# First pair of batches: copies of M1 on VectorE, two thirds of the early sums over w_in on GpSimd

## The chip, the cores and the metric

The kernel runs on one core of a Trainium2 chip. The core has a matrix engine (TensorE), three engines for elementwise work (VectorE, ScalarE, GpSimd) and a queue engine (SyncE); each works through its own list of instructions in order and waits on semaphores for the others. The metric is the device time of one execution in microseconds (us); smaller is better. The time shown is the median of repeated runs; the profile is of one further execution.

## The reference

The kernel computes an attention with a sigmoid in place of a softmax, and then a feed-forward block with SiLU:

```python
scores = q @ k.T / sqrt(64) - log(448)          # batch 8, heads 12, seq 448, head_dim 64
attn   = sigmoid(scores) @ v
x      = attn, heads side by side               # 3584 tokens x 768
h      = x @ w_in                               # w_in  768 x 2048
out    = (h * sigmoid(h)) @ w_out               # w_out 2048 x 768
```

Inputs and output are float32. The kernel works in float16 with float32 accumulation.

## The kernel before, in words

The order of the instructions is written out by hand; no scheduler moves them. What the program emits first on an engine runs first on that engine.

**Attention.** Batches are taken in pairs. A group `g` is a set of four heads of one batch (24 groups, three per batch). For each group `scores(g, ch)` (L210) computes one of seven chunks of scores in a double bank of PSUM (`psc`, two of them), and ScalarE turns it into `attnT` with a sigmoid. `values(g)` (L232) multiplies the seven chunks with v into two single banks (`pav`, from a pool of four), and VectorE moves them out as `xT`, scaled. k and q have to be transposed first: for groups 0 to 5 on TensorE, with copies by VectorE (`kT`, `qT`), later by DMA from copies `kr`, `qr`.

**Feed-forward.** For a pair of batches `h = x @ w_in` is a 2x2 block product by a seven-product scheme (Strassen's, Winograd's form): products M1 to M7 of sums of blocks of x (`tx`, by VectorE in `x_sums`, L336) and sums of blocks of w_in. The latter are four blocks, SI1, SI2, SI4 and SI3 (the last written over a block of w_in itself), each made in four quarters of its columns by `w_in_sums` (L318). `out` is made the same way, with sums over w_out (`w_sum`, L521), two of them by GpSimd behind a one-element copy (`gate`) that holds them until the last `tx` is there.

**The first pair.** The change lies here. The first 24 chunks of scores run with the work that the table `behind` places behind them. From chunk 24 on, `burst(n)` (L772) does two chunks of scores and, when a group is complete, its values; behind each burst `fill` takes a counted number of steps from `first_fill` (L603). Those steps are the part of the feed-forward that needs only the first batch: two plain columns (`h_unit`), then for columns 2 to 7 the products M1 and M2, then two plain columns again. M1 and M2 of one column share a bank: `early_m1` (L383) computes M1 and a copy of it is kept in `m1s` (L392), `early_m2` (L395) adds M2 on top, so M2 cannot start before the copy is done. Then ScalarE makes `sig` and VectorE writes `gTr` (`to_sig`, L278), which frees the bank. Between the bursts `next(in_sums)` emits one of the sums over w_in at a time, as `sums_behind` (L792) counts them: quarters 1, 2 and 3, twelve sums; quarter 0, whose columns are still needed, follows in `sets`, far later. After the last burst `last_part_of` (L803) begins the values of group 5 in new banks, and `first_pair` (L484) does the rest of the products.

**Loads.** All loads of q, k, v and weights go through GpSimd's queue (`load`, L112), in the order of the program: a load that has to wait for its buffer, or for one of eight transfers in flight, holds what stands behind it, loads and arithmetic alike. Buffers for groups are three deep, so k and q of group 8 take those of group 5. `after_transpose` (L679) and `after_values` (L691) say behind which step a load is emitted.

Of the kernel before, what the change touches and what calls it, by code (L numbers as in the profile page):

```python
# [13 lines left out]
AF = mybir.ActivationFunctionType  # L14
# [4 lines left out]
def kernel(  # L19
# [9 lines left out]
    nc = tc.nc  # L29
# [13 lines left out]
    NQB = NQ * B  # L43
# [41 lines left out]
    def one_bank(name):  # L85
        if "any" in banks:
            ring.append(ring.pop(0))
            return banks["any"].tile([P, 512], F32, tag=f"any{ring[-1]}", name=name)
        taken.append(name)
        return banks["single"].tile([P, 512], F32, tag="single", name=name)  # L90
# [12 lines left out]
    def new_flat(name, g):  # L103
        flat[name, g] = p3.tile([P, 2, NCH, D], F16, tag=f"{name}f", name=f"{name}f")

    def rows_in(name, g):
        b, iq = divmod(g, NQ)
        return source[name][b, 4 * iq : 4 * iq + 4].rearrange(
            "(i h) (p c) d -> (h p) i (c d)", h=2, c=NCH
        )  # L110

    def load(names, g, c0=0, c1=NCH):  # L112
        for name in names:
            if (name, g) not in flat:
                new_flat(name, g)
            nc.gpsimd.dma_start(  # L116
                flat[name, g][:, :, c0:c1].rearrange("p i c d -> p i (c d)"),
                rows_in(name, g)[:, :, c0 * D : c1 * D],
            )
# [144 lines left out]
    def first_col(m):  # L264
        return P if m % 2 == 0 else 0
# [12 lines left out]
    def to_sig(ph, to):  # L278
        if "sig" not in rooms:
            rooms["sig"] = [  # L280
                cpool.tile([P, 2, S], F16, tag=f"S{i}", name="sig") for i in range(1, 5)
            ]
            rooms["sig"] = [t[:, j] for j in range(2) for t in rooms["sig"]]
        tsig = rooms["sig"].pop(0)
        rooms["sig"].append(tsig)
        nc.scalar.activation(tsig, ph, AF.Sigmoid, bias=0.0, scale=ISX)
        nc.vector.scalar_tensor_tensor(  # L287
            out=to, in0=ph, scalar=ISX, in1=tsig, op0=ALU.mult, op1=ALU.mult
        )

    def h_unit(b, fc):
# [20 lines left out]
    wi = [  # L312
        [w_in_sb[:, c * NQ : (c + 1) * NQ, r * NH : (r + 1) * NH] for c in range(2)]
        for r in range(2)
    ]
    si = {3: wi[1][0]}

    def w_in_sums():  # L318
        for i in (1, 2, 4):
            si[i] = cpool.tile([P, NQ, NH], F16, tag=f"SI{i}", name=f"SI{i}")  # L320
        quarter = NH // 4
        add, sub = nc.vector.tensor_add, nc.vector.tensor_sub
        for at in (1, 2, 3, 0):
            cols = slice(at * quarter, (at + 1) * quarter)
            for op, o, x, y in (
                (add, si[1], wi[1][0], wi[1][1]),
                (sub, si[2], si[1], wi[0][0]),
                (sub, si[4], wi[0][1], si[2]),
                (sub, si[3], wi[0][0], wi[1][0]),
            ):  # L330
                op(o[:, :, cols], x[:, :, cols], y[:, :, cols])  # L331
                yield
# [19 lines left out]
    def products(m):  # L352

        x0 = xT[2 * m]
        col = first_col(m)
        bank, got = {}, {}

        def scratch():
            return p12.tile([P, S], F32, tag="attnT", name="part")

        def silu(i, r, c, h):
            nc.scalar.activation(  # L362
                gTr[:, r * NG + i, col + c * S : col + (c + 1) * S], h, AF.Silu, bias=0.0, scale=ISX
            )

        def steps(i, to, w, x, start=True):
            for n in range(NQ):
                nc.tensor.matmul(  # L368
                    to,
                    w[:, n, i * P : (i + 1) * P],  # L370
                    x[:, n],
                    start=(start and n == 0),
                    skip_group_check=not start,
                    stop=(n == NQ - 1),
                )
                if n < NQ - 1:
                    yield

        def product(*what, **how):
            for _ in steps(*what, **how):  # L380
                pass

        def early_m1(i):  # L383
            bank[i, "a"] = one_bank("pa")[:, :S]
            yield from steps(i, bank[i, "a"], wi[0][0], x0[:, :NQ])
            if "m1" not in rooms:
                rooms["m1"] = [
                    cpool.tile([P, NQ, 512], F32, tag=f"T{t}", name="m1s") for t in (2, 4)
                ]
                rooms["m1"] = [t[:, n, :S] for t in rooms["m1"] for n in range(NQ)]  # L390
            got[i, 1] = rooms["m1"].pop(0)
            nc.scalar.activation(got[i, 1], bank[i, "a"], AF.Copy)  # L392
            yield

        def early_m2(i):  # L395
            yield from steps(i, bank[i, "a"], wi[0][1], x0[:, NQ:], start=False)
            to_sig(bank[i, "a"], gTr[:, i, col : col + S])
            yield

        def plus(o, po, x):  # L400
            nc.vector.tensor_add(o, po, x)  # L401

        def m1(i):
            bank[i, "a"] = one_bank("pa")[:, :S]
            product(i, bank[i, "a"], wi[0][0], x0[:, :NQ])
            got[i, 1] = scratch()
            nc.scalar.activation(got[i, 1], bank[i, "a"], AF.Copy)  # L407

        def m2(i):
            product(i, bank[i, "a"], wi[0][1], x0[:, NQ:], start=False)  # L410

        def silu11(i):
            silu(i, 0, 0, bank[i, "a"])

        def m6(i):
            b = one_bank("pb")[:, :S]
            product(i, b, si[2], tx[m, 2])
            got[i, "u2"] = scratch()
            plus(got[i, "u2"], b, got.pop((i, 1)))

        def m5(i):
            bank[i, "d"] = one_bank("pd")[:, :S]
            product(i, bank[i, "d"], si[1], tx[m, 1])

        def m7(i):
            bank[i, "c"] = one_bank("pc")[:, :S]
            product(i, bank[i, "c"], si[3], tx[m, 3])
            got[i, "u3"], got[i, 22] = scratch(), scratch()
            plus(got[i, "u3"], bank[i, "c"], got[i, "u2"])

        def h22(i):
            plus(got[i, 22], bank[i, "d"], got.pop((i, "u3")))

        def m4(i):
            product(i, bank[i, "c"], wi[1][1], tx[m, 4], start=False)
            plus(bank[i, "c"], bank[i, "c"], got[i, "u2"])
            silu(i, 1, 0, bank[i, "c"])

        def m3(i):
            product(i, bank[i, "d"], si[4], xT[2 * m + 1][:, NQ:], start=False)  # L440
            plus(bank[i, "d"], bank[i, "d"], got[i, "u2"])
            silu(i, 0, 1, bank[i, "d"])

        def silu22(i):
            silu(i, 1, 1, got.pop((i, 22)))

        return SimpleNamespace(**locals())
# [231 lines left out]
    def after_transpose(g):  # L679
        if g == 0:  # L680
            load("kq", 3)
        elif g == 1:
            load("kq", 4)
            load_w_in(0)
            load_w_in(1)
        elif g == 2:
            load("kq", 5)
        elif g == 5:
            load("kq", 8)

    def after_values(g):  # L691
        if g == 0:
            load("v", 3)
            load_w_in(2)
            load_w_in(3)
        elif g == 1:
            load("v", 4)
            load_w_out(0, 0)
            load_w_out(0, 1)
        elif g == 2:  # L700
            load("v", 5)
            load_w_out(1, 0)
            load_w_out(1, 1)
            load("kq", 6)
            load("kq", 7)
        elif g + 3 < NQB:
            load("v", g + 3)
        if g % (2 * NQ) == 2 * NQ - 2:
            x_sums(g // (2 * NQ), 0, NQ - 1)
# [18 lines left out]
    def transposes(g, name):  # L728
        pe_transpose(g, ((name, 0, 4), (name, 4, NCH)))
        if name == "q":  # L730
            after_transpose(g)
# [53 lines left out]
    def fill(stream, n):  # L785
        for _ in range(n):
            next(stream, None)
# [1 line left out]
    first = products(0)  # L789
    stream = first_fill(first)  # L790
    behind_burst = {24: 6, 26: 4, 28: 4, 30: 4, 32: 7, 34: 7, 36: 4, 38: 7, 40: 3}
    sums_behind = {32: 2, 34: 2, 36: 3, 38: 3, 40: 2}  # L792
    fill(stream, 6)
    for n in range(NT_B + 3, 2 * NT_B, 2):
        burst(n)
        if n in (26, 30):
            transposes(5, "k" if n == 26 else "q")
        for _ in range(sums_behind.get(n, 0)):
            next(in_sums)
        fill(stream, behind_burst[n])  # L800
    assert next(stream, 0) == 0

    def last_part_of(g, m, then):  # L803
# [95 lines left out]
```

## Time and profile before

| | us |
|---|---|
| median of 3 runs | 385.35 (384.96 to 385.90) |
| profiled execution | 387.63 |
| its span, first to last instruction | 385.80 |
| TensorE busy | 365.8 (95%) |
| VectorE busy | 262.2 (68%) |
| ScalarE busy | 258.4 (67%) |
| GpSimd busy | 90.5 (23%) |

In the profile PE is TensorE, PEld its loading of weights, DVE VectorE, ACT ScalarE, POOL GpSimd and SP SyncE. A line such as `PE pa L368 <- ACT m1s L392: 3.4, 2, 1.9` says that TensorE, at line 368, waited for ScalarE's writing of m1s at line 392: 3.4 us in all, two times, the longest 1.9. Rows of a timeline give start, duration, engine, line, operation and its output and input. Where several instructions follow each other on one engine, the next often starts before the last has fully ended, so 0.55 us of duration can be 0.43 to 0.5 from start to start. Busy time of TensorE is not useful work as such: at half the granted clock the same products are busy for twice as long.

### The profile page before, as it was taken

What the parts mean: (1) busy time and instruction counts of PE and PEld (TensorE: products, weight loads), DVE (VectorE), ACT (ScalarE), POOL (GpSimd) and SP (SyncE); (2) the same over time, 40 slices, a digit from 0 to 9 for tenths busy, and PEclk for the clock granted to TensorE, in tenths of its full rate; (3) what the DMA queues carried; (4) which work ended last, traced back from release to release, by engine and by line L of the source; (5) the groups of instructions that cost most, each with busy time, mean ns of one, the idle gap of its engine ahead of it and who ended that gap; (6) DMA issues with size and microseconds to landing.
All of it is one profiled execution on the core that took longest, in us unless ns stands there. A gap on an engine that the chain in (4) does not pass through costs nothing.

```text
span 385.8 us, 7628 instructions
## 1 busy us (share of the span) xinstructions
PE 365.8 (95%) x2991; PEld 181.7 (47%) x2991; DVE 262.2 (68%) x476; ACT 258.4 (67%) x352; POOL 90.5 (23%) x125
## 2 busy tenths in 40 slices
PE   7997777999999999989999999999999999999995
PEld 3553323454444445544444455554444445555553
DVE  2663664799766658785765678787656658797763
ACT  5999980589888956667777765669898856650000
POOL 8567321854006035100005007200000000000000
PEclk9999986999999999999999999999999999999999
DMA  8999999178998859900967958920785020002333
GB/s 140 201 203 204 204 204 148 24 143 127 175 116 150 151 116 115 150 13 5 174 130 109 212 109 109 162 41 2 141 119 122 3 82 3 0 2 63 87 96 82
DMA packets 65700, 42.80 MB, mean 111 GB/s; under 512 B 36096, under 2 KB 62208, under 8 KB 65664
## 3 DMA queue, kind: packets, MB, share of 16 engines
q0 software_dynamic: 27072, 22.58, 40.8%
q1 hardware_dynamic: 38240, 19.44, 26.4%
q8 instruction: 23, 0.38, 0.4%
q10 hardware_dynamic: 352, 0.30, 0.2%
q14 instruction: 13, 0.11, 0.1%
HBM read 45.61 MB, written 11.01 MB: 147 GB/s over the span
## 4 chain that ended last, share of the span: by engine, by line
PE 81%; ACT 10%; DVE 5%; issue 3%; ACTq 0%; DVEq 0%
PE po L558 30%; PE psc L217 9%; PE pav L246 9%; PE pc L368 8%; PE pd L368 8%; PE pa L368 8%; ACT attnT L224 7%; PE pb L368 4%; PE ph L295 2%; ACT gTr L362 2%; PE pw L175 1%; DVE SI L331 1%; DVE gTr L287 1%; DVE xT L257 1%; DVE kT L195 1%
## 5 line engine op out<-in xcount | busy, mean ns | idle before, releaser
L224 ACT ACTIVATE attnT<-psc,bias_s 128x896 f16<-128x896 f32 x168 | 159.1, 1008 | 26.2 <-PE psc L217 25.6
L217 PE MATMUL psc<-qT,kT 64*64 64x448 f16 x672 | 55.3, 366 | 3.3 <-ACT attnT L224 1.8
L558 PEld LDWEIGHTS <-S 128*128 128x128 f16 x448 | 40.7, 98 | 36.8 <-issue 10.0
L257 DVE TENSOR_SCALAR xT<-pav 128x448 f16<-128x448 f32 x48 | 27.7, 619 | 40.0 <-PE pav L246 40.0
L368 PEld LDWEIGHTS <-w_in_sb 128*128 128x128 f16 x360 | 34.1, 98 | 36.8 <-issue 6.4
L116 POOL DMA_DIRECT2D vf<-in_v_dram x24 | 17.2, 717 | 142.7 <-PE pav L246 135.7
L246 PE MATMUL pav<-attnT,vf 64*64 64x448 f16 x672 | 42.0, 367 | 5.1 <-DVE gTr L287 5.0
L368 PE MATMUL pa<-xT,w_in_sb 128*128 128x448 f16 x180 | 41.9, 353 | 3.7 <-ACT m1s L392 3.4
L558 PEld LDWEIGHTS <-gTr 128*128 128x128 f16 x336 | 30.8, 98 | 29.0 <-issue 11.0
L558 PE MATMUL po<-w_out_sb,gTr 128*128 128x384 f16 x224 | 42.3, 327 | 1.4 <-ACT gTr L362 1.4
L558 PE MATMUL po<-T,S 128*128 128x384 f16 x224 | 42.5, 327 | 0.3 <-DVE S L569 0.3
L558 PE MATMUL po<-w_out_sb,S 128*128 128x384 f16 x224 | 40.4, 327 | 0.0
L368 PEld LDWEIGHTS <-SI 128*128 128x128 f16 x270 | 26.4, 98 | 25.1 <-issue 0.7
L217 PEld LDWEIGHTS <-kT 64*64 64x64 f16 x672 | 18.0, 104 | 38.4 <-issue 34.9
L246 PEld LDWEIGHTS <-vf 64*64 64x64 f16 x672 | 22.6, 111 | 19.2 <-issue 11.2
L368 PE MATMUL pc<-tx,w_in_sb 128*128 128x448 f16 x108 | 26.3, 352 | 0.3 <-DVE part L401 0.3
L407 ACT ACTIVATE part<-pa 128x448 f32<-128x448 f32 x24 | 13.1, 544 | 20.1 <-PE pa L368 20.0
L362 ACT ACTIVATE gTr<-pc 128x448 f16<-128x448 f32 x30 | 16.3, 543 | 13.3 <-DVE pc L401 12.8
L362 ACT ACTIVATE gTr<-part 128x448 f16<-128x448 f32 x30 | 17.2, 575 | 9.6 <-DVE part L401 9.6
L401 DVE TENSOR_TENSOR part<-pc,part 128x448 f32<-128x448 f32 x30 | 18.6, 622 | 6.3 <-PE pc L368 5.5
L558 PE MATMUL po<-T,gTr 128*128 128x384 f16 x112 | 22.2, 327 | 0.0
L368 PE MATMUL pb<-tx,SI 128*128 128x448 f16 x90 | 21.9, 352 | 0.0
(83 smaller groups left out, 468.0 us busy)
## 6 DMA issues: line engine op xcount, KB each, us to landing
out_dram<-osb SPq DMA_DIRECT2D x54, 192.0 KB, 2.9
vf<-in_v_dram POOLq DMA_DIRECT2D x24, 224.0 KB, 6.3
kf<-in_k_dram POOLq DMA_DIRECT2D x23, 224.0 KB, 7.1
qf<-in_q_dram POOLq DMA_DIRECT2D x23, 224.0 KB, 8.7
w_in_sb<-in_moe_w_in_dram POOLq DMA_DIRECT2D x16, 192.0 KB, 7.9
w_out_sb<-in_moe_w_out_dram POOLq DMA_DIRECT2D x4, 768.0 KB, 14.9
kT<-kr SPq DMA_TRANSPOSE x18, 3.1
qT<-qr SPq DMA_TRANSPOSE x18, 3.8
```

The costliest lines, as they stand in the source:

```text
L116: nc.gpsimd.dma_start(flat[name, g][:, :, c0:c1].rearrange("p i c d -> p i (c d)"), rows_in(name, g)[:, :, c0 * D : c1 * D],)
L175: nc.tensor.matmul(pw, dummy[:, :P], dummy, start=True, stop=True)
L217: nc.tensor.matmul(psc[own, j, :S], qkT["k", g][rows, ch, own], qkT["q", g][rows, :, own], start=True, stop=True,)
L224: nc.scalar.activation(attnT[g, ch], psc[:, :, :S], AF.Sigmoid, bias=bias_s, scale=QKSCALE)
L246: nc.tensor.matmul(pav[half][j * D : (j + 1) * D, :S], flat["v", g][own, j, ch, :], at[own, j, :], start=(ch == 0), stop=(ch == NCH - 1),)
L257: nc.vector.tensor_scalar_mul(xT[b][:, half * NQ + iq, :], pav[half][:, :S], SX)
L295: nc.tensor.matmul(ph, w_in_sb[:, cc, fc * P : (fc + 1) * P], xT[b][:, cc, :], start=(at == 0), stop=(at == NCC - 1),)
L362: nc.scalar.activation(gTr[:, r * NG + i, col + c * S : col + (c + 1) * S], h, AF.Silu, bias=0.0, scale=ISX)
L368: nc.tensor.matmul(to, w[:, n, i * P : (i + 1) * P], x[:, n], start=(start and n == 0), skip_group_check=not start, stop=(n == NQ - 1),)
L401: nc.vector.tensor_add(o, po, x)
L407: nc.scalar.activation(got[i, 1], bank[i, "a"], AF.Copy)
L558: nc.tensor.matmul(po[:, :NO2], a[:, fc, :], w[:, fc, :], start=(fc == 0), stop=(fc == NHC - 1))
```

## The change

Three things change, all for the first pair of batches.

- `early_m1`: the six copies of M1 are made by VectorE, not by ScalarE.
- `w_in_sums`: of the twelve sums amid the bursts, the four of quarter 1 stay on VectorE and the eight of quarters 2 and 3 go to GpSimd; quarter 0, later, stays on VectorE. The counts behind the bursts change from 2, 2, 3, 3, 2 (behind chunks 32 to 40) to 2 and 10 (behind chunks 34 and 36).
- Loads: k and q of group 8, emitted behind the transposes of group 5 before, are emitted between GpSimd's two quarters; v of groups 6 and 7, emitted behind the values of groups 3 and 4 before, follow after the last burst.

```diff
-        add, sub = nc.vector.tensor_add, nc.vector.tensor_sub
-        for at in (1, 2, 3, 0):
+        for at, eng in ((1, nc.vector), (2, nc.gpsimd), (3, nc.gpsimd), (0, nc.vector)):
             cols = slice(at * quarter, (at + 1) * quarter)
             for op, o, x, y in (
-                (add, si[1], wi[1][0], wi[1][1]),
-                (sub, si[2], si[1], wi[0][0]),
-                (sub, si[4], wi[0][1], si[2]),
-                (sub, si[3], wi[0][0], wi[1][0]),
+                (eng.tensor_add, si[1], wi[1][0], wi[1][1]),
+                (eng.tensor_sub, si[2], si[1], wi[0][0]),
+                (eng.tensor_sub, si[4], wi[0][1], si[2]),
+                (eng.tensor_sub, si[3], wi[0][0], wi[1][0]),
             ):
...
             got[i, 1] = rooms["m1"].pop(0)
-            nc.scalar.activation(got[i, 1], bank[i, "a"], AF.Copy)
+            nc.vector.tensor_copy(got[i, 1], bank[i, "a"])
             yield
...
         elif g == 2:
             load("kq", 5)
-        elif g == 5:
-            load("kq", 8)
...
-        elif g + 3 < NQB:
+        elif 4 < g < NQB - 3:
             load("v", g + 3)
...
-    sums_behind = {32: 2, 34: 2, 36: 3, 38: 3, 40: 2}
+    sums_behind = {34: 2, 36: 10}
...
-        for _ in range(sums_behind.get(n, 0)):
+        for i in range(sums_behind.get(n, 0)):
+            if i == 6:
+                load("kq", 8)
             next(in_sums)
         fill(stream, behind_burst[n])
+    load("v", 6)
+    load("v", 7)
     assert next(stream, 0) == 0
```

## The prediction

> **What bounds the kernel now.** I read the page's slices first, then the chain of waits and TensorE's waits in the stretch that the diff touches, then the timelines of VectorE and GpSimd there.
>
> ```profile
> PE   7997777999999999989999999999999999999995
> PEclk9999986999999999999999999999999999999999
> ```
>
> Slices are 9.6 us. TensorE is full nearly everywhere after slice 8; the holes are slices 3 to 6 (29 to 67 us), where the first pair's scores, values and early products run, and there the granted clock falls too. The change acts only there. After that everything is one chain through TensorE, so what is won by 68.8 us (the first `pd` product) should reach the end.
>
> TensorE's waits from 28 to 70 us:
>
> ```profile
> PE pav L246 <- DVE gTr L287: 5.0, 2, 4.6
> PE pa L368 <- ACT m1s L392: 3.4, 2, 1.9
> ```
>
> Both are waits that the diff addresses: 3.4 us behind the copies of M1 on ScalarE (1.45 at 32.8, 1.91 at 47.4), and one of 4.6 us before the last values, until VectorE frees a bank. The chain in order of time says why:
>
> ```profile
> 45.11 1.80 ACT attnT L224 x2
> 46.91 0.44 ACT m1s L392
> 47.40 0.35 PE pa L368
> ...
> 54.04 0.62 DVE tx L350
> 54.66 0.48 DVE SI L331
> 55.16 0.57 DVE SI L331
> 55.75 0.56 DVE SI L331
> 56.31 0.53 DVE gTr L287
> 56.85 0.46 DVE w_in_sb L331
> 57.31 0.48 DVE SI L331
> 57.81 0.56 DVE SI L331
> 58.37 0.54 DVE gTr L287
> 58.91 0.47 DVE SI L331
> 59.37 0.47 DVE w_in_sb L331
> 59.84 0.55 DVE gTr L287
> 60.43 2.45 PE pav L246 x21
> ```
>
> A copy of M1 stands behind two sigmoids of scores on ScalarE. And the `gTr` that frees the bank stands behind eight sums over w_in on VectorE (4.05 us of these pieces), though its own input, the last `sig`, ended at 57.07.
>
> **The change part by part.** Durations are of the one profiled execution: span 385.80 and 1.83 around it, 387.63 in all, which is 2.3 above the median of 385.35. I take the difference from the median.
>
> *Copies of M1.* ScalarE loses six instructions of 0.55 us (m1s, L392), 0.43 from start to start: 2.6 us. It is full from 27.5 to 47.8 but for gaps of 0.58 and 0.70. VectorE gets six copies; nearest rows, `xT<-pav` at 0.62 (same size, from PSUM) and `m<-po` 128x384 at 0.56; so 0.62 each, 3.7 us, in 28 to 50 us where it is busy 10.4 of 22. Behind a copy on VectorE stand a cast of `kT` and the `gTr`s, for which TensorE waits 0.3, 0.4 and 0.2 us now; each may come 0.5 later, which is covered as long as the copy itself starts earlier than on ScalarE. At 32.8: the matmuls of the second M1 end at 31.3, VectorE is free at 31.06, so TensorE goes on at about 31.6; but the next scores need the bank of the sigmoid that ends at 32.28, so the burst behind comes 0.9 earlier. At 47.4: four more copies would give ScalarE 4 x 0.43 = 1.7; but ScalarE already waits for TensorE's scores there (0.58, 0.55 us), so I take 0.6 of it. Together 1.5; ends 0.9 (the first place alone) and 2.6 (all ScalarE time).
>
> *Eight sums to GpSimd, four others later.* VectorE loses eight of 0.55 us. Of the four that stay, SI4 and w_in_sb move from 45.7 behind the `tx` subtractions. So with the start as it is: `tx` ends 54.66, two sums to 55.6, `gTr` to 56.1, `gTr` to 56.7, and the last waits for its `sig` (57.07) and ends 57.73 in place of 60.38. The bank is free 2.65 us earlier. What is late next is that sigmoid on ScalarE, which moves with the 1.5 above. Ends: 2.65, and 1.7 if the six copies push VectorE's casts back by 0.5 twice.
>
> *On GpSimd:* eight sums at 1.64 us (its own row, `T<-w_out_sb` 128x768 f16) are 13.1 us. Its timeline:
>
> ```profile
> 45.03 0.72 POOL L116 DMA_DIRECT2D qf<-in_q_dram  x1 [3.12 <-DMA w_out_sb<-in_moe_w_out_dram]
> 49.10 0.72 POOL L116 DMA_DIRECT2D vf<-in_v_dram  x1 [3.35 <-PE psc L217]
> 54.49 0.72 POOL L116 DMA_DIRECT2D qf<-in_q_dram  x1 [3.78 <-PE psc L217]
> 66.13 0.72 POOL L116 DMA_DIRECT2D vf<-in_v_dram  x1 [7.42 <-PE pav L246]
> 68.52 6.44 POOL L531 TENSOR_TENSOR T<-w_out_sb 128x768 f16<-128x768 f16 x4
> ```
>
> Behind the q of group 7 (issued to 45.75) stand four sums to 52.3, then k and q of group 8 (49.99 and 54.49 now) at 52.3 and 53.0, four sums to 60.3, then v of 6, 7 and 8 at 60.3 to 62.5 (49.10, 57.99, 66.13 now). The sums are first read by the `pb` products of columns 4 and 6, at 73.9 and 79.6 now, at 70 and 75.7 then: 15 us to spare. Group 8's rows are copied from 81.5, v of 6 is used near 98, and loads land in 6 to 9 us: 15 and 30 us to spare. The w_out sums, at 68.52 now, follow a gate on the last `tx`, near 64.4 then; GpSimd is free at 62.5. So these cost nothing; cover lost, each us beyond that delays the second T set (ends 82.15, read by VectorE at 88.34, 6 us to spare), and only then the product on it. SP's queue issues nothing in this stretch; its transposes at 76 only shift.
>
> *VectorE beside GpSimd.* Eight adds of VectorE with both operands in SBUF (`SI`, `tx`) would now meet GpSimd's sums. The trace of before has no such pair: beside GpSimd's `T` sums from 70 to 82 VectorE ran only adds with one operand in PSUM, 0.62 us as without them. Bounds: 0 (that row), and a wait until GpSimd's stretch of four sums ends. For the upper one: `tx` would begin at 52.35 in place of 50.8, all `gTr` be done 52.35 + 2.25 + 0.95 + 1.65 = 57.2, in place of 56.2: 1.0; if the stretch begins a sum later, 2.2 to 2.6. I take 0, by the only row there is.
>
> [...]
>
> *Clock.* It is granted at 0.50 from 47.9 to 51.1 and from 58.0 to 64.6. TensorE still stands from the end of the last H product to that bank, about 55.8 to 57.7 less the shift, 1.9 us; the 1.9 us wait before 47.4 was followed by the first half-clock stretch, so by that row it closes again. Resuming earlier inside a closed stretch costs up to 1.2 more (a stretch of 3.3 us at half speed costs 1.65); if it stays open, 8.3 us from 60.4 to the first `pd` become 5.8 (24 products at 0.19 and 26 `pav` at 1.32 for 28), a gain of up to 2.5, and as much as 1.3 at 48 to 51 (`pav` 2.66 for 28, 1.32 elsewhere). I take 0.3 of loss. [...]
>
> Sum: -1.5 - 2.65 + 0 + 0.3 = -3.85, so 385.35 - 3.85 = 381.5 (profiled: span near 382.0).
>
> **Rivals.** *The two engines take turns in SBUF* (above). For: both streams read SBUF only, and fall in the same 46 to 60 us; against: no row of it. 1.0 to 2.2 given back: 382.5 to 383.7, say 383.0.
>
> *Hidden anyway.* ScalarE's time is taken by waits for scores, copies push VectorE back, and the clock closes for two stretches: 0.9 + 1.7 - 1.2 leaves 1.4 at best, and less where the next bank wait is longer: 384.5. For: ScalarE's own waits of 0.55; against: the sums' 4 us stand on the chain, piece by piece.
>
> *Slower: VectorE's adds lose every turn to GpSimd's sums.* Place: the four `tx`, SI4 and w_in_sb behind the fourth values. Price: one whole sum each, 6 x 1.64 = 9.8 us, less the 4.15 won: 391. It decides from 4.15 us of delay, that is, when `gTr` frees the bank after 60.4; so three adds losing a turn are enough. Against: GpSimd has only four sums before it issues two loads, 1.4 us in which VectorE runs.
>
> **How the numbers follow.** No contention to speak of: 0.46; turns in SBUF: 0.29, of which 0.02 end within 0.3%; hidden: 0.13, of which 0.11 within 0.3% and 0.02 beyond; slower: 0.12. 0.3% is 1.2 us, about what separates a change from none in this kernel. Faster 0.46 + 0.27 + 0.02 = 0.75, same 0.13, slower 0.12. The range: low 381.5 - 2.4 for a clock that stays open and 0.6 of further ScalarE time, 378.5; high to the hidden case, 384.6; some 0.8 lies inside.
>
> **What would show it.** Right: no wait of `pa` for m1s over 1 us; `pav` of the last group waits for `gTr` under 2.5 us, with the last `gTr` directly behind its `sig`; the first `pd` near 65. Turns in SBUF: `tx` or `SI` rows on VectorE far over 0.62, or idle before them, while GpSimd sums run, and GpSimd's over 1.64. Wrong: half clock through more than the two stretches of now, the wait before the last values at 4 us or more, `pb` waiting for GpSimd, or rows of group 8 waiting for their load.

## The result, and the profile after

The changed kernel is slower: 391.41 us (391.14 to 391.88) against 385.61 (384.96 to 385.90), a ratio of 1.0154 with a 95% interval of 1.0136 to 1.0172. The prediction of 381.5 (378.5 to 384.6) was wrong, and on the wrong side.

First TensorE's slices and its granted clock, from the page of the changed kernel (40 slices, tenths):

```profile
PE   7998764999999999989999999999999999999995
PEclk9999985999999999999999999999999999999999
```

The hole is where it was and has become deeper: its last slice, from 58 us, stands at 4 and 5 in the two rows, 7 and 6 before. TensorE's waits from 28 to 80 us (total, times, longest):

```profile
PE pav L246 <- DVE gTr L287: 9.7, 2, 9.3
PE pa L367 <- DVE m1s L391: 2.3, 3, 1.4
```

The wait for copies of M1 fell from 3.4 to 2.3 us, as it should. The wait for VectorE before the last values, which was to fall under 2.5 us, doubled from 4.6 to 9.3. The chain of waits in order of time says what is in it (start, us, what):

```profile
46.35 0.35 PE pa L367
...
49.90 1.14 DVE xT L257 x2
51.04 0.57 DVE tx L346
...
51.63 1.94 DVE tx L347
53.58 3.08 DVE tx L348
56.66 1.97 DVE tx L349
58.63 1.91 DVE SI L330
60.53 1.91 DVE w_in_sb L330
62.44 1.61 DVE gTr L287 x3
64.05 0.04 issue
64.09 2.45 PE pav L246 x22
```

The eight sums are gone from this list, but five of the six adds that stayed take 1.9 to 3.1 us each, where the same instructions took 0.5 to 0.6. They are shown as busy, not as waiting. GpSimd's timeline shows what ran beside them (start, us, engine, line, operation):

```profile
45.31 0.71 POOL L116 DMA_DIRECT2D qf<-in_q_dram  x1 [3.13 <-DMA w_out_sb<-in_moe_w_out_dram]
46.05 1.65 POOL L330 TENSOR_TENSOR SI<-w_in_sb 128x768 f16<-128x768 f16 x1
...
51.08 2.02 POOL L330 TENSOR_TENSOR w_in_sb<-w_in_sb 128x768 f16<-128x768 f16 x1
53.05 0.74 POOL L116 DMA_DIRECT2D kf<-in_k_dram  x1
53.78 0.72 POOL L116 DMA_DIRECT2D qf<-in_q_dram  x1
54.51 1.65 POOL L330 TENSOR_TENSOR SI<-w_in_sb 128x768 f16<-128x768 f16 x1
56.24 1.91 POOL L330 TENSOR_TENSOR SI<-SI,w_in_sb 128x768 f16<-128x768 f16 x1
58.23 1.90 POOL L330 TENSOR_TENSOR SI<-w_in_sb,SI 128x768 f16<-128x768 f16 x1
60.08 1.95 POOL L330 TENSOR_TENSOR w_in_sb<-w_in_sb 128x768 f16<-128x768 f16 x1
```

Read the two lists side by side: one add of VectorE ends about 0.5 us after each sum of GpSimd, at 53.6, 56.7, 58.6, 60.5 and 62.4; and most of GpSimd's sums beside them take 1.9 to 2.0 us in place of 1.65. The two engines alternate. VectorE's instructions without a second operand in SBUF are not touched by it: in its timeline beside the first of these sums they take 0.61 and 0.62 us, as they did just before it (0.61 to 0.62, from 43.02 on):

```profile
45.68 0.62 DVE L391 COPY m1s<-pa 128x448 f32<-128x448 f32 x1
46.21 0.61 DVE L287 SCALAR_TENSOR_TENSOR gTr<-pa,sig 128x448 f16<-128x448 f32 x1
```

So the bank came free at 64.05 in place of 60.38. Of the 5.8 us between the medians, 3.6 stand between the two profiled spans (385.8 and 389.4). Most of the other 2.2 is in the profiled execution of before, one of its longer ones: 387.63 for a median of 385.61.

### The profile page after: what moved, and what is told of

Same layout as the page of the kernel before. It is cut to its first block, busy times and chain, and to the rows that moved or that the text cites. A ratio compares the mean times of both kernels' runs of the same rounds, so it can differ in the third digit from the quotient of the medians.

```text
span 389.4 us, 7625 instructions
## 1 busy us (share of the span) xinstructions
PE 365.7 (94%) x2991; PEld 181.5 (47%) x2991; DVE 269.4 (69%) x474; ACT 255.8 (66%) x346; POOL 104.8 (27%) x133
## 4 chain that ended last, share of the span: by engine, by line
PE 80%; ACT 8%; DVE 8%; issue 3%; ACTq 0%; DVEq 0%
PE po L557 30%; PE psc L217 9%; PE pav L246 9%; PE pc L367 8%; PE pd L367 8%; PE pa L367 8%; ACT attnT L224 6%; PE pb L367 4%; PE ph L295 2%; PE pw L175 1%; DVE gTr L287 1%; ACT gTr L361 1%; DVE tx L348 1%; DVE SI L330 1%; DVE part L400 1%
## 5 line engine op out<-in xcount | busy, mean ns | idle before, releaser
L367 PE MATMUL pd<-xT,SI 128*128 128x448 f16 x90 | 21.9, 352 | 0.2 <-DVE part L400 0.2
```

The source lines that it names most:

```text
L367: nc.tensor.matmul(to, w[:, n, i * P : (i + 1) * P], x[:, n], start=(start and n == 0), skip_group_check=not start, stop=(n == NQ - 1),)
```

## The experiments

The theory after the traces: adds of VectorE with two operands in SBUF and GpSimd's sums hold each other up, and VectorE's queue carries that to the bank that TensorE waits for. Rivals: the copies on VectorE; the later loads, or ten sums behind one burst; sums on GpSimd as such, wherever they stand. Each kernel ran on one chip beside the kernel before, whose medians there were 385.8 to 387.5 us; differences below are to that median, where nothing else is said. The row "loads behind the sums" has only three executions of before beside it (385.90, 387.52, 387.64), so its ratio is the least certain.

| | time, us | ratio to before, 95% |
|---|---|---|
| copies alone | 385.31 | 0.9982 (0.9966 to 0.9998) |
| sums and loads alone | 391.50 | 1.0141 (1.0125 to 1.0157) |
| the change, all sums on VectorE | 386.73 | 1.0010 (0.9995 to 1.0024) |
| copies, and sums late on VectorE | 382.55 | 0.9914 (0.9895 to 0.9934) |
| sums late, copies on ScalarE | 382.19 | 0.9913 (0.9885 to 0.9941) |
| the change, GpSimd fills | 383.53 | 0.9916 (0.9887 to 0.9945) |
| the change, GpSimd copies | 386.93 | 1.0019 (0.9991 to 1.0047) |
| the change, loads behind the sums | 391.13 | 1.0106 (1.0046 to 1.0166) |
| four sums on GpSimd, after the last `tx` | 381.61 | 0.9864 (0.9825 to 0.9902) |
| late sums, last H column first | 380.56 | 0.9841 (0.9812 to 0.9870) |
| both of these | 379.79 | 0.9826 (0.9800 to 0.9853) |

### One part alone

The kernel before, with only this line changed:

```diff
-            nc.scalar.activation(got[i, 1], bank[i, "a"], AF.Copy)
+            nc.vector.tensor_copy(got[i, 1], bank[i, "a"])
```

> Only the copies of M1 move to VectorE; sums and loads stay as before. If the loss comes from VectorE and GpSimd taking turns in SBUF, this part is a small gain: in the trace of the changed kernel the fourth values began 1.3 us earlier (47.0 for 48.4), so 0.5 to 1.5 us faster than before, and the wait before the last values stays near 4.6 us, since the sums still stand before the last gTr. If the copies on VectorE are what hurts, slower by 2 us or more.

Measured: 0.8 us faster (0.1 to 1.3 by the interval). The longest wait of `pa` fell from 1.91 to 1.3, and that of `pav` for `gTr` stayed at 4.6. The copies are a small gain, not the loss.

The other half, the change with that one line put back:

> Only the sums and the loads change; the copies stay on ScalarE. If the two engines take turns, the whole loss is here and somewhat more than in the changed kernel: 6 to 8 us slower than before, with six VectorE adds of 1.9 to 3.2 us instead of 0.6. If the copies are to blame, within 1 us of before.

Measured: 5.4 us slower, nearly as much as both together, and less than the 6 to 8 expected: beside the sums on GpSimd the copies gain nothing that shows. `pav` waits 9.8 us for `gTr`. Seven adds of VectorE take 1.9 to 3.0 us here, the first of them from 44.98, 0.6 us before GpSimd's first sum (45.59) begins in the profile:

```profile
44.98 2.68 DVE L330 TENSOR_TENSOR SI<-w_in_sb 128x768 f16<-128x768 f16 x1
47.69 1.88 DVE L330 TENSOR_TENSOR SI<-SI,w_in_sb 128x768 f16<-128x768 f16 x1
```

So the loss lies in the sums and the loads.

### The same order, without GpSimd

```diff
-        for at, eng in ((1, nc.vector), (2, nc.gpsimd), (3, nc.gpsimd), (0, nc.vector)):
+        for at, eng in ((1, nc.vector), (2, nc.vector), (3, nc.vector), (0, nc.vector)):
```

> The changed kernel in everything (copies, counts behind the bursts, order of the loads) but with all twelve sums on VectorE. If taking turns is the cause, adds are back at 0.55 to 0.62 us and the loss is gone: 1 us faster than before to equal. If the later loads, or ten sums behind one burst, are the cause, it stays 4 us or more slower than before.

Measured: equal to before (1.0010, 0.9995 to 1.0024). Every add is back at 0.55 to 0.62 us, and `pav` waits 5.7 us for `gTr`, since now ten sums stand between the `tx` and it, two more than before. From VectorE's timeline:

```profile
50.58 0.62 DVE L347 TENSOR_TENSOR tx<-xT,tx 128x896 f16<-128x896 f16 x1
51.13 0.62 DVE L348 TENSOR_TENSOR tx<-xT 128x896 f16<-128x896 f16 x1
```

Order and counts are the changed kernel's, so they don't cost 4 us; GpSimd's part does. The loads are emitted where the changed kernel has them, but without sums ahead of them they are issued earlier (those of group 8 between 47 and 51 us, where GpSimd is busy for 1.43 us with two instructions); the kernel with fills below, which issues them at 51.92 and 52.63 where the changed kernel does at 53.05 and 53.78, shows that their being late is not the cost either.

### What in GpSimd's work blocks

Two kernels put something else in the place of each of the eight sums and so leave the sums of quarters 2 and 3 out. First fills, which write and do not read:

```diff
+                if eng is nc.gpsimd:
+                    nc.gpsimd.memset(o[:, :, cols], 0.5)
+                    nc.gpsimd.memset(o[:, :, cols], 0.5)
+                else:
+                    op(o[:, :, cols], x[:, :, cols], y[:, :, cols])
```

> The changed kernel with each of GpSimd's eight sums left out and two fills of the same tile in its place (GpSimd writes SBUF but reads nothing; the sums of quarters 2 and 3 are left out). If VectorE's two-input adds lose time to GpSimd's reads alone, the adds beside the fills stay at 0.55 to 0.65 us and the time falls to 382 to 384.5 us. If any GpSimd instruction blocks them, they stretch as in the changed kernel and the time is 389 us or more.

Measured: 383.53 us, with a wait of 2.0 us for `gTr`. VectorE's timeline, and then GpSimd's, over the same stretch:

```profile
51.76 0.62 DVE L351 TENSOR_TENSOR tx<-xT,tx 128x896 f16<-128x896 f16 x1
...
53.37 0.55 DVE L334 TENSOR_TENSOR SI<-w_in_sb,SI 128x768 f16<-128x768 f16 x1
53.84 0.55 DVE L334 TENSOR_TENSOR w_in_sb<-w_in_sb 128x768 f16<-128x768 f16 x1
```

```profile
51.23 0.74 POOL L332 MEMSET w_in_sb<- 128x768 f16 x1
...
53.34 0.77 POOL L331 MEMSET SI<- 128x768 f16 x1
54.16 0.74 POOL L332 MEMSET SI<- 128x768 f16 x1
```

Beside fills the same adds take what they take alone (0.55 and 0.62 us), and the fills take 0.74 to 0.77 us beside them, 0.73 to 0.74 behind them. Then two copies in place of each sum (`tensor_copy` of `x`, then of `y`):

> The changed kernel with each of GpSimd's eight sums left out and two copies from SBUF in its place, one input each (about 0.8 us each by the rows of 128x896). If one read stream is enough to block VectorE's two-input adds, each add waits for copies of 0.8 us, half a sum, and the time is 386 to 389 us. If only a two-input GpSimd instruction blocks, adds stay at 0.62 and the time is 382 to 384.5 us.

Measured: 386.93 us, inside the range expected of one read stream. It includes a second loss: the first two adds of w_in (1.77 and 1.06 us) now hold up a copy of M1, for which TensorE waits 3.1 us. VectorE's timeline:

```profile
54.25 1.13 DVE L351 TENSOR_TENSOR tx<-xT,tx 128x896 f16<-128x896 f16 x1
55.30 1.24 DVE L352 TENSOR_TENSOR tx<-xT 128x896 f16<-128x896 f16 x1
56.46 1.24 DVE L353 TENSOR_TENSOR tx<-xT,tx 128x896 f16<-128x896 f16 x1
```

and GpSimd's:

```profile
54.95 1.11 POOL L332 COPY SI<-w_in_sb 128x768 f16<-128x768 f16 x1
56.12 1.10 POOL L331 COPY SI<-SI 128x768 f16<-128x768 f16 x1
```

The add waits for a copy of 0.83 where it waited for a sum of 1.64, and is stretched by 0.5 to 0.6 where it was stretched by 1.3 to 1.4: what it pays goes with the length of the GpSimd instruction that it meets, and is 0.2 to 0.3 us less. So in these runs it is GpSimd's reading of SBUF that blocks an add with two operands there; one read stream is enough, and writing alone does not count: an add of 0.62 alone takes 0.62 us beside fills, 1.1 to 1.2 beside copies and 1.9 to 2.1 beside sums.

### Whether loads between the sums leave an opening

The prediction counted on the two loads of group 8 as 1.4 us in which VectorE runs freely.

The changed kernel, with both loads behind all eight sums:

```diff
-        for i in range(sums_behind.get(n, 0)):
-            if i == 6:
-                load("kq", 8)
+        for _ in range(sums_behind.get(n, 0)):
             next(in_sums)
         fill(stream, behind_burst[n])
+    load("kq", 8)
     load("v", 6)
```

> The changed kernel with the two loads of group 8 behind all eight of GpSimd's sums instead of between the two fours. If the loads between them leave VectorE an opening, as the prediction had it, taking them away costs: each of the six adds waits a sum, and the last gTr comes no earlier than in the changed kernel (63.5 us). If the loads only lengthen the wait of the add that meets them (3.2 us there, 1.9 to 2.0 for the others), that add falls to about 2 us and the last gTr comes 1 to 1.4 us earlier, time 390 us.

Measured: 391.13 us, as long as the changed kernel (391.41). VectorE's timeline:

```profile
50.12 2.00 DVE L346 TENSOR_TENSOR tx<-xT 128x896 f16<-128x896 f16 x1
52.16 1.94 DVE L347 TENSOR_TENSOR tx<-xT,tx 128x896 f16<-128x896 f16 x1
54.02 2.05 DVE L348 TENSOR_TENSOR tx<-xT 128x896 f16<-128x896 f16 x1
55.99 2.05 DVE L349 TENSOR_TENSOR tx<-xT,tx 128x896 f16<-128x896 f16 x1
```

Now all six adds take 2 us, and none 3. The last `gTr` ends 0.6 us earlier than in the changed kernel, not 1.0 to 1.4: the adds began 0.8 us earlier, but the first of them, which slipped through there, met a sum here. So the loads gave no opening: in the changed kernel the add issued at 53.50, beside them, ended only after the sum behind them. That it is the loads that stretched it by another microsecond fits, but the total does not tell it apart from the shift. In the profile of before, a load's issue at 41.19 does not stretch the adds at 41.18 and 41.76 (0.55, 0.56), so it isn't the issue of a load alone. "Sums and loads alone" has two more such adds, from 44.98 and from 53.18: both begin beside a load's issue, 0.6 and 0.9 us before a sum of GpSimd begins in the profile, and both end only 0.4 to 0.5 us after that sum:

```profile
53.18 3.04 DVE L347 TENSOR_TENSOR tx<-xT,tx 128x896 f16<-128x896 f16 x1
```

```profile
54.08 1.65 POOL L330 TENSOR_TENSOR SI<-w_in_sb 128x768 f16<-128x768 f16 x1
```

So an add that would have ended before the sum's shown start can be held until after it. With copies in place of the sums such an add is held by only 0.3 us (from 53.27, 0.94 us, the copy from 54.04). Whether the sum begins earlier than shown, or the loads ahead of it take part, stays open.

### Where the sums cost nothing

If the sums stood before the last `gTr` in before, and meeting is what costs after, they belong behind it. VectorE idled 5.4 us there, between that `gTr` and the last `xT`.

The kernel before, with the copies on VectorE, and:

```diff
-    sums_behind = {32: 2, 34: 2, 36: 3, 38: 3, 40: 2}
+    sums_behind = {32: 2, 34: 2}
...
         fill(stream, behind_burst[n])
+    for _ in range(8):
+        next(in_sums)
```

> Before, with the copies on VectorE and the eight sums of quarters 2 and 3 emitted behind the last burst, on VectorE, behind the last gTr. If the wait before the last values is what the sums cost in before, it falls from 4.6 to about 2 us, and the sums fit between the last gTr and the last xT, where VectorE idles 5.4 us in before: 3 to 6 us faster than before. If that wait is set by something else, 1 us faster, as the copies alone.

Measured: 382.55 us, 3.6 us faster than before. The wait for `gTr` is 2.0 us, and the last `gTr` stands directly behind its `sig`: the 2.65 us that the prediction worked out for this term are there, without GpSimd. From VectorE's timeline:

```profile
54.43 0.62 DVE L287 SCALAR_TENSOR_TENSOR gTr<-ph,sig 128x448 f16<-128x448 f32 x1 [1.37 <-ACT sig L286]
```

The same with the copies back on ScalarE:

> Only the late sums, with the copies of M1 on ScalarE as in before. Splits the gain of the late version: if the two parts add up, 2.2 to 3 us faster than before, with the wait before the last values near 2 us; if the copies are what let the late sums gain, 1 us faster or equal.

Measured: 382.19 us, the same wait of 2.0 us, and 3.6 us faster than before: somewhat above the expected 2.2 to 3. The two medians do not differ by more than their runs scatter (381.5 to 383.8, and 382.1 to 384.5), so the gain of the copies, 0.8 us alone, can't be seen on top of this one.

Then the late version with the four sums of quarter 3 back on GpSimd, but behind the gate on the last `tx`, ahead of the sums over w_out:

```diff
-    for _ in range(8):
+    for _ in range(4):
         next(in_sums)
...
             nc.gpsimd.tensor_copy(gate, tx[m, 4][:1, NQ - 1, :1])
+            if m == 0:
+                for _ in range(4):
+                    next(in_sums)
```

> The late version, with the four sums of quarter 3 on GpSimd behind the last tx, where VectorE has no add with two SBUF inputs for 20 us. If it is the meeting of the two streams that costs, and not sums on GpSimd as such, the time is that of the late version within 1 us (382 to 383.5 us), and the sums take 1.65 us each. If sums on GpSimd cost as such (a load behind them, a product waiting for them), 385 us or more.

Measured: 381.61 us, slightly below the expected 382 to 383.5 and no slower than the late version. GpSimd's timeline:

```profile
63.84 0.18 POOL L814 COPY gate<-tx 1x1 f16<-1x1 f16 x1 [1.53 <-DVE tx L349]
63.99 1.63 POOL L330 TENSOR_TENSOR SI<-w_in_sb 128x768 f16<-128x768 f16 x1
65.70 1.64 POOL L330 TENSOR_TENSOR SI<-SI,w_in_sb 128x768 f16<-128x768 f16 x1
```

The same instruction on the same engine takes 1.63 to 1.65 us and hinders nobody: VectorE then comes to adds with one operand in PSUM, and the first of them, at 65.56, takes 0.62 us. In before such adds take 0.61 to 0.62 us beside GpSimd's sums over w_out (from 70 to 82 us) and the same behind them. The rival that sums on GpSimd cost as such falls.

### A version that beats both

Of the 2 us that are left of the wait, the last `sig` spends about 1.0 behind two sigmoids of scores on ScalarE, by the profile of before: its products end at 55.5, the two sigmoids take 1.92 us from 54.72, and it begins at 56.50. The late version with copies on VectorE, and with the last three steps of the last plain column moved ahead of the last burst:

```diff
-    behind_burst = {24: 6, 26: 4, 28: 4, 30: 4, 32: 7, 34: 7, 36: 4, 38: 7, 40: 3}
+    behind_burst = {24: 6, 26: 4, 28: 4, 30: 4, 32: 7, 34: 7, 36: 4, 38: 10}
...
-        fill(stream, behind_burst[n])
+        fill(stream, behind_burst.get(n, 0))
```

> The late version with the last three steps of the last plain column behind the burst of chunk 38 in place of 40, so that its sig goes ahead of two sigmoids of scores on ScalarE. If the 2 us that are left of the wait before the last values are that queueing on ScalarE, the wait goes under 0.5 us and the time is 1 to 3 us below the late version (379.5 to 381.5 us, with the clock open more often). If ScalarE's last scores then come later by as much, the same 382.5 us.

Measured: 380.56 us, inside the expected range. The wait fell to 1.1 us, not under 0.5: VectorE now comes to that `gTr` 0.4 us after its `sig`, and takes 0.6 for it. TensorE's waits:

```profile
PE pa L368 <- DVE m1s L392: 2.2, 3, 1.3
PE pav L246 <- DVE gTr L287: 1.4, 2, 1.1
```

With the four sums of quarter 3 on GpSimd as well:

> The same with the four sums of quarter 3 on GpSimd behind the last tx. The sums are off VectorE in a stretch where it has time, so the same as with all sums late on VectorE, within 1 us; more than 1 us slower if GpSimd's sums over w_out, pushed back by 6.6 us, are then waited for.

Measured: 379.79 us, within 1 us of the run before as expected and the lowest median of all, 6.6 us below before and 11.6 below the median of the changed kernel. Its distance to the run before, 0.8 us, lies inside the two intervals.

## Why the prediction was wrong

**Copies of M1: right in sign, half in size.** 1.5 was taken, 0.8 measured. The wait at 32.8 went as worked out (TensorE goes on at 31.51, predicted 31.6), but the second place still waits 1.4 us, now for a copy that stands on VectorE behind the sums and a `gTr`. That is the lower end, 0.9. In the changed kernel even that does not show: without the copies it takes 391.50, with them 391.41.

**The sums off VectorE's queue: right as a term, not reached.** 2.65 us were to come from the bank. The late versions show that the term is there, and so do the fills: in both the wait for `gTr` is 2.0 us. In the changed kernel it was more than eaten by the next one.

**VectorE beside GpSimd: the step that failed.** The prediction took 0 of loss, "by the only row there is", a row of adds with one operand in PSUM. It had noted that the adds concerned have both in SBUF and that no row of before shows such a pair; the row chosen was of another kind of instruction, and so no bound at all. The upper end was also too small: it let each add wait at most until the stretch of four sums ends (1.0 to 2.6 us in all), with the loads as an opening. An add that waits out the sum it meets, each time, is the rival at 391. What happens is that each add pays for a sum and lets the next one go first: six adds took 11.8 us where they take 3.6 alone, 8.2 more. The slower rival had this mechanism and place, and a price near it (9.8 us, 391 us), and got a chance of 0.12; the reason that held it down, that the loads would let VectorE through, is what the runs refute. That its 391 lies so close to 391.41 is in part luck: its delay is 1.6 us too large, and of the gain of 4.15 that it takes off, the 1.5 of the copies did not show.

**Sums and loads on GpSimd: right in what they cost, up to 1.7 us early in time.** The sums began at 46.05 and 54.51, the loads of group 8 were issued at 53.05, v of 6 at 61.97; no product waited for a sum, and no row for its load.

**Clock: small between the two profiles, larger against the median.** The prediction took 0.3 of loss. In the changed kernel the clock is at half from 47.0 to 50.5 and from 57.3 to 67.5, in before from 47.8 to 51.2 and from 58.0 to 64.8; but up to 64.1 and 60.4 TensorE waits and loses nothing by it. Of half clock on a working TensorE 6.8 us are left, against 7.8 in before, so between these two executions the clock gives back some 0.5. What the sum left out is that the profiled execution of before was itself longer than most by the clock: the terms were worked out on it, and then taken off the median. The last section has the size of that, about 1.7.

## What to carry to other kernels

In these runs an add of VectorE with two operands in SBUF and a GpSimd instruction that reads SBUF took turns: an add of 0.62 us took 1.1 to 1.2 beside copies of 0.83, and 1.9 to 2.1 beside sums of 1.64. So work moved from VectorE to GpSimd should run beside other instructions of VectorE: here those with an operand in PSUM kept their 0.6 us. A row of that kind says nothing about the other kind. Look for the meeting in durations, not in waits: a blocked instruction was shown as busy, for 1.9 to 3.2 us. Before giving work to a slower engine (a sum took 1.64 us on GpSimd, 0.55 on VectorE), look whether it can stand later in the same queue: here the idle 5 us behind the instruction that everyone waited for held all of it.

## What the runs showed of the hardware that was not expected

The alternation is strict: in the kernel with the loads behind the sums, where GpSimd's sums follow each other without a break, six adds in a row took 1.94 to 2.05 us each (0.55 to 0.62 alone), and the five sums that began beside them 1.89 to 2.02 (1.64 alone). Neither engine got two in a row.

The granted clock moves in steps that can be seen in the executions' times. Of 23 executions of the kernel before on one chip, 20 had a mean granted clock of 0.991 and spans of 383.5 to 384.8, three had 0.986 or 0.987 and 385.8 to 386.0: about 1.7 us, what a stretch of 3.4 us at half speed costs. The profiled execution of before was of the second kind; the changed kernel was at 0.981 or 0.982 in all four. Worked out from these means, that is two stretches of half clock in most executions of before, three in the profiled one and four in the changed kernel; the two profiles show three and four, as 3.4 and 6.8 us in before and as 3.4 and 10.2 in the changed kernel. Of its four, two cost nothing, since TensorE waits in them. So it is the missing third stretch in most executions of before that makes up most of the 2.2 us that the two profiles do not show.
